# First block in four plain units, the second block's attention in the loop: a rewritten opening

## The chip, the cores and the metric

The kernel runs on one core of a Trainium2 chip. The metric is the device time of one execution in microseconds. Such a core has TensorE (PE, with weight loads listed apart as PEld), VectorE (DVE), ScalarE (ACT), GpSimd (POOL) and SyncE (SP), which here only issues the transfers of the DMA engines.

## What is computed

Attention over windows, and then two expert layers, all in float32. The core of the reference:

```python
for c in range(768 // 32):                       # windows of 32 queries, 16 left, 8 right
    k_full = concat([mem_k, k[:, :, l_start:r_end]])
    scores = scale * q_c @ k_full.T;  a = exp(scores - max);  a = a / (sum(a) + 1e-9)
    out[:, :, c_start:c_end] = a @ concat([mem_v, v_ctx])
x = out.reshape(3072, 512)                       # 4 batches x 768 tokens, 8 heads x 64
h = x @ w_in;  x = (h * sigmoid(1.702 * h)) @ w_out               # 512 -> 2048 -> 512
out = (silu(x @ w_gate) * (x @ w_val)) @ w_out2                   # 512 -> 1536 -> 512
```

The weights come as 64-bit floats and are turned into float32 on the chip.

## The kernel before

**Tiles.** The 3072 tokens are six blocks of 512, each of four groups of 128. Attention goes by group: queries (256 KB), keys and values with their windows laid out (512 KB each). The layers go by block and unit: a unit of the first layer is 256 columns of its hidden size (eight units), one of the second layer 128 (twelve). Every matrix product is made three times in float32r, with operands split into a high and a low half (high x high, high x low, low x high).

**A unit.** `unit` makes the two 128-column parts of a unit with seven products of 256 columns instead of eight (sums of weights `s12`, `s34` and of tokens stand in for the eighth). A plain unit (`plain_up`) makes them with two banks of twelve products of 512 columns and needs no token sums, but the untouched weights `a`, `a21`, `v`. After the gate, `down` adds the unit's part of the output in four steps `d`, six products of 512 columns each.

**Order of blocks.** `seq` gives each layer two passes over all blocks. In the first pass of the first layer block 0 takes two units (`PLAIN`) and each other block four; the second pass takes the rest. Units 0 to 3 stay in SBUF for the whole first pass. From `n = 2` on, the loop spreads the attention of the next block over the four units (`PLACES`); a unit's down steps run inside the next units (`chunk`).

**The opening.** Until the loop's first unit all engines and SP's queue follow a hand-written order, the string `OPENING`. A name is a step and a number: `ldq`, `ldk`, `ldv`, `ldw` load queries, keys, values and raw weight blocks; `sc`, `mx`, `ex`, `sm`, `ra`, `rc`, `wg`, `te`, `ec`, `pv`, `xf`, `st` are the attention of a group, scores to store; `hi` and `xl` split its result; `pr`, `cs`, `ct` turn a raw block into float32 (ScalarE, then two steps on VectorE); `wa`, `wb`, `wv`, `wo` cast high halves on ScalarE and the names with `l` behind them make low halves on GpSimd; `sumA`, `sumB`, `hiA`, `loA`, `hiB`, `loB` make the sums of weights and split them. `ua`, `ub` are the two half passes (six products of twelve) of a plain bank; `th`, `gt`, `gc`, `rs` are its gate; `dn`, `dm` the down steps of units 0 and 1. `tc`, `tl`, `ts` split and sum the tokens of block 1. The old opening also writes out units 0 to 2 of block 1 in seven products (`qa` to `qg` and the rest), and the attention of groups 0 to 11. Each engine runs its own names in that order; a DMA that waits for a buffer holds up all that is behind it on SP.

**Buffers.** Raw blocks (512 KB) 0 to 2 and from 7 on take any free one of three buffers (`RB`), blocks 3 to 6 lie in spare weight slots. Block 1, 3, 9 and 13 also hold the sums of their unit until these are split. A unit's blocks are {0, 1; 4, 5}, {2, 3; 6, 7}, {8, 9; 10, 11}, {12, 13; 14, 15}. Before, the keys of groups 0 to 7 have eight buffers of their own (`k_open`); later groups share `kbd`, so their load waits for the scores of the group ahead.

**Weights later.** New weights are made a step at a time between products; `pace` divides the steps left by the slots until a unit is due, and `give_w` frees slots after a unit's last use (`final`).

Of the kernel before, what the change touches and what calls it, by code (L numbers as in the profile page):

```python
# [19 lines left out]
P = 128  # L20
# [23 lines left out]
PLAIN = 2  # L44
# [13 lines left out]
def tile_attention_moe_moe(  # L58
# [198 lines left out]
    def split_lo(w, f, o=0, n=512):  # L257
        nc.gpsimd.tensor_sub(w[:, 1, o : o + n], f, w[:, 0, o : o + n].bitcast(F32))  # L258
# [24 lines left out]
    nraw, bits = [2 * len(AT)], {}  # L283
# [79 lines left out]

    ready = {(1, u) for u in range(2 * PLAIN)}

    def all_weights():
        for ph in (1, 2):
            for u in range(2 * PLAIN if ph == 1 else 0, UNITS[ph]):
                yield from weight_steps(ph, u)
        yield None  # L370

    weights = all_weights()
    need, made = [next(weights)], [40 * PLAIN]
# [16 lines left out]
    class Tokens:  # L390
# [10 lines left out]
        def sum(self, k):  # L401

            eng = self.engs[7 + k]
# [246 lines left out]
    SPARE = 14  # L650
# [6 lines left out]
    v_open = vm + [spare[12].bitcast(F32).rearrange("p (a c d) -> p a c d", a=HP, c=4)]  # L657
    ebd.append(spare[13].bitcast(F32).rearrange("p (a c e q) -> p a c e q", a=HP, c=4, e=2))
# [6 lines left out]
    def load_q(g):  # L665
        if g >= 2 * GRP or g % GRP < 2:
# [19 lines left out]
    def load_kv_first(n, g):  # L686
        if g >= 2 * GRP:
# [6 lines left out]
    def scores_first(g):  # L694
        if g >= 2 * GRP:
            at["k", g] = scores(g)
            return
# [10 lines left out]
    def exponents_first(g):  # L708
        if g >= 2 * GRP:
# [7 lines left out]
    def values_first(g):  # L717
        at["x", g] = values(g, bank("ps_v"), vm[g % 2] if g >= 2 * GRP else v_open[g % 3])
# [15 lines left out]
    def lo_x(g):  # L734
        eng, src = (V, at["x", g]) if g == GRP - 1 else (G, xq[g])
# [43 lines left out]
    def down_first(d):  # L779
        if "y" not in psum:  # L780
            s_ctx.close()
            psum["y"] = pool("ps_y", 1, PSUM)
        down(1, 0, 0, True, False, firsts[0], None, None, d, 0.5)

    def down_second(d):
        down(1, 0, 1, False, True, firsts[1], None, None, d, 0.5, held=full)

    full = {}

    def evict_first(d):  # L790
        full[d] = evict(full[d], None, d, 0.5)

    def store_first(d):
        nc.sync.dma_start(out=yp[0][:, d, :], in_=full.pop(d))

    seconds, un = [[] for _ in range(3)], [{} for _ in range(3)]
    QN = BLK // 2

    def quarter(bank_, part):
        return lambda u: un[u][bank_][:, part * QN : part * QN + QN]  # L800

    ca0, ca1, cb0, cb1 = quarter("a", 0), quarter("a", 1), quarter("b", 0), quarter("b", 1)

    def unit_product(new, out, w, o, k):
        def f(u):
            if new:
                un[u][new] = bank(f"ps_{new}")
            key, off = ((1, u, w), o) if w != "v" else ((1, u - u % 2, "v"), u % 2 * HALF)
            product(out(u), wt[key], off, tokens().ops[k], start=out is cb1 and k == 2 or new is not None)

        return f

    def unit_copy(name, src):
        def f(u):
            un[u][name] = cpool.tile([P, QN], F32, tag=name, name=name)
            nc.scalar.copy(un[u][name], src(u))

        return f

    def unit_add(out, name, src):  # L820
        return lambda u: V.tensor_add(out(u), un[u][name], src(u))  # L821

    def unit_curve(bank_):
        return lambda u: un[u].update({"t" + bank_: curve(un[u][bank_], 1)})

    def unit_gate(bank_):
        return lambda u: gate(un[u][bank_], un[u].pop("t" + bank_), un[u][bank_])

    def unit_cast(bank_):
        return lambda u: seconds[u].append(cast(un[u][bank_]))  # L830

    def unit_rest(bank_):
        return lambda u: rest(un[u][bank_], seconds[u]["ab".index(bank_) ^ 1])

    def unit_down(d):
        return lambda u: down(1, 1, u, u == 0, False, seconds[u], None, None, d, 0.5)

    def tokens():
# [29 lines left out]
        "wal": lambda u: split_lo(wt[1, u, "a"], bits[IN[u]]),  # L868
# [5 lines left out]
        "wbl": lambda u: split_lo(wt[1, u, "a21"], bits[IN[u] + 1][:, :HALF], 0, HALF),  # L874
# [233 lines left out]
```

## Time and profile before

| | |
|---|---|
| time, median of 3 runs | 1189.48 us (1189.32 to 1191.52) |
| the profiled execution's own time | 1190.33 us |
| its span, first to last instruction | 1188.6 us |
| TensorE busy | 1151.3 us (97%) |
| VectorE, ScalarE, GpSimd busy | 652.1, 568.1, 354.9 us |
| mean granted TensorE clock | 0.991 |

Times are from the span's start. A busy TensorE is not TensorE at its peak: products overlap, so the spacing of starts tells more than the mean duration. The clock is a share of full speed.

### The profile page before, as it was taken

How to read it: one execution, taken by the hardware profiler on the slowest of the kernel's cores; microseconds unless marked ns; L12 is line 12 of the kernel's file. 1: busy time of each engine (PE TensorE's matmuls, PEld its weight loads, DVE VectorE, ACT ScalarE, POOL GpSimd, SP SyncE). 2: the span in 40 equal slices, each digit the busy share in tenths (PEclk: the TensorE clock that was granted, in tenths of full speed). 3: DMA queues.
4: the chain of work that ended last, by engine and by line, in shares of the span. 5: the costliest groups of instructions: out<-in, count | busy, mean ns of one | idle time of the engine just before them, and what ended most of it. 6: DMA issues, size and time to landing. Idle time of an engine off the chain costs nothing.

```text
span 1188.6 us, 22301 instructions
## 1 busy us (share of the span) xinstructions
PE 1151.3 (97%) x8908; PEld 1039.6 (87%) x8908; DVE 652.1 (55%) x1117; ACT 568.1 (48%) x1185; POOL 354.9 (30%) x321
## 2 busy tenths in 40 slices
PE   4889999999999999999999999999999999999998
PEld 3778888888989999999988989999999999999997
DVE  5886756565765444443466564453556554453553
ACT  4866555455565454444455544343445544243342
POOL 4564221202454232321235433021345521021010
PEclk9889999999999999999999999999999999999999
DMA  9977354441454313322333321210225130320302
GB/s 304 296 253 231 110 157 120 130 140 63 137 166 118 106 66 114 131 74 62 106 116 107 106 99 36 72 71 1 89 89 178 36 103 5 107 92 15 107 25 83
DMA packets 62920, 131.47 MB, mean 111 GB/s; under 512 B 5728, under 2 KB 26208, under 8 KB 60512
## 3 DMA queue, kind: packets, MB, share of 16 engines
q1 hardware_dynamic: 62816, 130.05, 34.9%
q8 instruction: 70, 1.15, 0.4%
q14 instruction: 34, 0.28, 0.1%
HBM read 98.57 MB, written 31.46 MB: 109 GB/s over the span
## 4 chain that ended last, share of the span: by engine, by line
PE 86%; DMA 5%; DVE 3%; ACT 2%; issue 2%; POOL 1%; SPq 0%; DVEq 0%; ACTq 0%; POOLq 0%
PE y L585 35%; PE ps_a L450 27%; PE ps_c L450 12%; PE ps_b L450 9%; DMA raw<-in_wr 2%; PE ps_s L201 1%; PE ps_o L174 1%; DMA q<-in_qg 1%; DMA w<-in_kg 1%; DMA xd<-xf 1%; PE ps_t L158 1%; PE ps_v L174 1%; ACT ebd L167 0%; PE ps_u L546 0%; ACT g L551 0%
## 5 line engine op out<-in xcount | busy, mean ns | idle before, releaser
L450 PEld LDWEIGHTS ps_a<-b,w 128*128 128x128 f32 x2832 | 384.3, 189 | 39.6 <-DVE ps_a L502 4.2
L450 PE MATMUL ps_a<-b,w 128*128 128x256 f32 x2832 | 397.5, 283 | 5.7 <-DVE ps_a L502 2.1
L585 PE MATMUL y<-gs,w 128*128 128x512 f32 x1152 | 298.6, 395 | 0.6 <-DVE gs L565 0.5
L585 PE MATMUL y<-w,gs 128*128 128x512 f32 x864 | 247.7, 395 | 0.6 <-DVE gs L565 0.5
L585 PEld LDWEIGHTS y<-gs,w 128*128 128x128 f32 x1152 | 204.2, 189 | 36.2 <-DVE gs L565 1.4
L450 PE MATMUL ps_c<-b,w 128*128 128x256 f32 x1224 | 179.1, 282 | 0.0
L450 PEld LDWEIGHTS ps_c<-b,w 128*128 128x128 f32 x1224 | 167.1, 190 | 8.8
L585 PEld LDWEIGHTS y<-w,gs 128*128 128x128 f32 x864 | 144.2, 190 | 14.4 <-DVE gs L565 1.7
L258 POOL TENSOR_TENSOR w<-wf,w 128x512 fp32r<-128x512 f32 (+1 forms) x68 | 78.3, 1152 | 222.0 <-ACT w L255 221.9
L450 PE MATMUL ps_b<-b,w 128*128 128x256 f32 x900 | 135.5, 287 | 1.7 <-DVE ps_b L821 1.2
L450 PEld LDWEIGHTS ps_b<-b,w 128*128 128x128 f32 x900 | 120.4, 193 | 5.9 <-issue 1.7
L553 ACT ACTIVATE g<-ps_b 128x512 f32<-128x512 f32 x72 | 43.1, 598 | 166.1 <-DVE ps_b L508 166.1
L436 DVE TENSOR_TENSOR b<-xl,b 128x512 fp32r<-128x512 f32 x72 | 64.3, 893 | 80.4 <-ACT b L432 80.3
L502 DVE TENSOR_TENSOR ps_a<-m,ps_a 128x256 f32<-128x256 f32 x115 | 48.9, 426 | 104.0 <-PE ps_a L450 98.0
L492 ACT COPY u<-ps_a 128x256 f32<-128x256 f32 x115 | 43.0, 373 | 107.8 <-PE ps_a L450 107.6
L415 POOL TENSOR_TENSOR xl<-xl,t 128x512 f32<-128x512 f32 x18 | 23.3, 1296 | 231.3 <-DVE t L412 230.0
L565 DVE TENSOR_TENSOR gs<-ps_a,gs 128x512 fp32r<-128x512 f32 x118 | 80.8, 685 | 10.2 <-ACT gs L561 9.8
L487 DVE TENSOR_TENSOR ps_b<-p,ps_b 128x256 f32<-128x256 f32 x115 | 49.2, 427 | 61.3 <-PE ps_b L450 54.0
L561 ACT CAST gs<-ps_a 128x512 fp32r<-128x512 f32 x118 | 69.8, 592 | 22.5 <-DVE ps_a L531 15.6
L531 DVE TENSOR_TENSOR ps_a<-g,ps_a 128x512 f32<-128x512 f32 x72 | 50.0, 694 | 45.7 <-PE ps_a L450 45.2
L483 ACT COPY p<-ps_a 128x256 f32<-128x256 f32 x115 | 43.0, 374 | 60.3 <-PE ps_a L450 56.4
L508 DVE TENSOR_TENSOR ps_b<-u,ps_c 128x256 f32<-128x256 f32 x102 | 43.5, 426 | 50.1 <-PE ps_c L450 49.8
(123 smaller groups left out, 1190.6 us busy)
## 6 DMA issues: line engine op xcount, KB each, us to landing
raw<-in_wr SPq DMA_DIRECT2D x49, 512.0 KB, 3.4
xl<-yd SPq DMA_DIRECT2D x12, 1024.0 KB, 4.8
vm<-in_vg SPq DMA_DIRECT2D x22, 512.0 KB, 6.0
kbd<-in_kg SPq DMA_DIRECT2D x32, 256.0 KB, 4.2
raw<-in_wr SPq DMA_DIRECT2D x30, 256.0 KB, 5.3
yp<-o SPq DMA_DIRECT2D x24, 256.0 KB, 3.8
xl<-xd SPq DMA_DIRECT2D x6, 1024.0 KB, 4.8
base<-yp SPq DMA_DIRECT2D x24, 256.0 KB, 3.4
```

The costliest lines, as they stand in the source:

```text
L258: nc.gpsimd.tensor_sub(w[:, 1, o : o + n], f, w[:, 0, o : o + n].bitcast(F32))
L436: self.engs[k].tensor_sub(x[:, 1], self.source(k), x[:, 0].bitcast(F32))
L450: nc.tensor.matmul(ps, w[:, a, o + kc * P : o + kc * P + P], x[:, c, kc, :], start=(start and kc == 0 and (a, c) == PASSES[0]), stop=(kc = ...
L483: nc.scalar.copy(p1, ca[:, :n])
L487: add(cb[:, :n], p1, cb[:, :n])
L502: add(ca[:, n:], m, ca[:, :n])
L508: add(cb[:, n:], u2, cc)
L531: late[0] = [lambda: nc.vector.tensor_mul(ca, t, ca), lambda: gs.append(cast(ca))]
L553: nc.scalar.activation(t, c, AF.Silu)
L561: nc.scalar.copy(x[:, 0], g)
L565: nc.vector.tensor_sub(x[:, 1], g, x[:, 0].bitcast(F32))
L585: nc.tensor.matmul(y, lhs, rhs, start=(first and o == 0 and (a, c) == PASSES[0]), stop=(ends and o == len(gs) - 1 and (a, c) == passes[-1]),)
```

## The change

Block 0 takes four plain units in its first pass, all in the opening. Block 1's units all run in the loop, where `n = 1` now carries the attention of block 2 (groups 8 to 11). The opening keeps the attention of groups 0 to 7, all sixteen raw blocks and the weights of units 0 to 3, and ends where unit 0 of block 1 begins, with the token operands of block 1 split. Groups 4 to 7 take the later form of attention, with `kbd` and `vm` shared. Names can carry `/V` or `/G`: VectorE or GpSimd in place of the usual engine. The `a21` weights of two units share a tile, and the spare slots fall from 14 to 10.

```diff
-PLAIN = 2
+PLAIN = 4
...
-    spare_raw = [t.bitcast(I64) for t in spare[:4]]
+    spare_raw = [t.bitcast(I64) for t in spare[5:9]]
...
-    k_open += [spare[6 + i].bitcast(F32).rearrange("p (a c k) -> p a c k", a=HP, c=4) for i in range(6)]
+    k_open += [spare[i].bitcast(F32).rearrange("p (a c k) -> p a c k", a=HP, c=4) for i in range(2)]
...
     def load_kv_first(n, g):
-        if g >= 2 * GRP:
+        if g >= GRP:
...
     def scores_first(g):
-        if g >= 2 * GRP:
+        if g >= GRP:
...
-    def lo_x(g):
-        eng, src = (V, at["x", g]) if g == GRP - 1 else (G, xq[g])
+    def lo_x(g, eng=None):
+        src = at["x", g] if g == GRP - 1 else xq[g]
+        eng = eng or (V if g == GRP - 1 else G)
...
     def split_b(u):
-        wt[1, u, "a21"] = bpool.tile([P, 2, HALF], F32R, tag="b", name="a21")
-        split_hi(wt[1, u, "a21"], bits[IN[u] + 1][:, :HALF], 0, HALF)
+        if u % 2 == 0:
+            wt[1, u, "a21"] = wt[1, u + 1, "a21"] = bpool.tile([P, 2, BLK], F32R, tag="b", name="a21")
+        part_b(u, split_hi)
...
-    def down_second(d):
-        down(1, 0, 1, False, True, firsts[1], None, None, d, 0.5, held=full)
...
+            down(1, 0, u, u == 0, False, firsts[u], None, None, d, 0.5)
...
+        "dn": down_first(0),
+        "dm": down_first(1),
+        "do": down_first(2),
...
     OPENING = """
...
+        z0 tb0 z1 ldq0 ldk0 ldk1 ldq1 ldq2 ldv0 ldv1 ldk2 ldk3 sc0 ldq3 ldv2 mx0 sc1 ldq4 ex0 mx1 z2 ldw0 ldq5
+        sm0 ex1 sm1 ra0 sc2 rc0 ra1 wg0 ldw1 rc1 te0 wg1 mx2 te1 ec0 ldk4 sc3 ex2 ec1 sm2 pv0 mx3 ra2 pr0 ldw2
+        ex3 cs0 pv1 ldv3 ct0 xf0 hi0 st0 rc2 sm3 wg2/G wa0 ldw3 ra3 pr1 rc3 wg3 xl0 te2 xf1 cs1 hi1 st1 te3 ct1
+        ec2 ldw4 wal0 sc4 xl1/V wb0 pv2 ec3 sumA0 mx4 ldk5 pr2 wbl0 pv3 ldw5 hi2 sumB0 ldq6 xf2 hi3 xl2 cs2 hiB0
+        ua0 xl3 wv0 st2 pr3 ct2 ldv4 wvl0 xf3 ub0 ldv5 ex4 loB0 cs3 ldw6 wa1 ct3 ua1 th0 wal1/V sumA1 wv1 wb1
+        gt0 ua2 ldw7 pr4 st3 sm4 sumB1 gc0 ub1 ra4 rs0 pr5 ldw8 wbl1 cs4 hiA1 ub2 rc4 hiB1 wvl1 ct4 th1 loB1 cs5
+        ldw9 ua3 wo0 ct5 th2 wol0 gt1 wo1 sc5 gt2 gc1 wol1 ub3 pr6 ldk6 rs1 gc2 cs6 wg4/G ldq7 dn0 pr7 rs2 th3
+        ct6 te4 hiA0 cs7 dn1 wo2 loA0 mx5 ec4 wol2 dn2 ct7 pr8 gt3 wo3 ldw10 pv4 cs8 wol3 gc3 ct8 pr9 dn3 ldv6
+        rs3 wa2 ldw11 cs9 xf4 sc6 wal2 ct9 ex5 st4 dm1 ldq8 sm5 wv2 sumA2 ldk7 wb2 mx6 ra5 dm2 pr10 sumB2 hiA2
+        rc5 ua4 ex6 wg5 wbl2 hiB2 cs10 te5 pr11 wvl2 loB2/V ub4 loA2 ec5 cs11 ldw12 ct10 ua5 th4 ct11 ldw13 wo4
+        gt4 sc7 wo5 wol4 ldw14 sm6 gc4 ub5 ldk8 mx7 ra6 wol5 dm0 rc6 ex7 rs4 wg6/G th5 sm7 pv5 pr12 gt5 ra7 dm3
+        cs12 ldv7 gc5 rc7 xf5 rs5 wg7/G te6 pr13 st5 ct12 do1 ec6 cs13 ldw15 ct13 te7 pr14 do2 loA1/V wv3 sumA3
+        ec7 pv6 wvl3 wb3 pv7 tc0 wbl3 ldv8 xf6 tl0/V sumB3 ua7 xf7 ldv9 st6 tc1 ts0/G st7 do0 pr15 tl1/V wa3 ts1
+        ub7 wal3/V hiA3 hiB3 cs14 ua6 ts2/G ct14 th7 cs15 wo6 loB3 ct15 ub6 gt7 wo7 wol6 wol7/V tc3 th6 tl3/G
+        tc2 gt6 tl2/V gc6 loA3 gc7 rs6 ts3/G rs7 tc5 tl5 tc4 tl4/V tc6 tl6
     """
...
-    late[0] = [lambda: unit_rest("b")(2), lambda: unit_gate("a")(2)]
...
-        steps = attention(b + 1) if attends and n > 1 else []
+        steps = attention(b + 1) if attends and n else []
...
-            if n == 1 and u < 3:
-                gs = seconds[u]
-            elif n:
+            if n:
                 gs = unit(ph, u, ops, chunk, after, n < NBLK - 1, ph == 1 and ua > 0, nxt is None and last)
```

## Rows read from the trace of the kernel before

**Rows 1.** The page's first two parts: TensorE, its clock, the DMA engines.

```profile
PE 1151.3 (97%) x8908; PEld 1039.6 (87%) x8908; DVE 652.1 (55%) x1117; ACT 568.1 (48%) x1185; POOL 354.9 (30%) x321
...
PE   4889999999999999999999999999999999999998
...
PEclk9889999999999999999999999999999999999999
```

**Rows 2.** Windows: stretch, length, busy us of each engine, clock, DMA share, GB/s.

```profile
2.00:28.00 26.00, 10.49 (x369) 8.57 (x372) 14.23 (x27) 11.52 (x26) 9.32 (x11) 0.97 1.05 323
28.00:70.00 42.00, 36.37 (x622) 29.69 (x607) 36.21 (x58) 32.58 (x66) 25.94 (x26) 0.86 1.04 318
70.00:85.00 15.00, 12.07 (x95) 10.23 (x91) 11.10 (x15) 7.22 (x16) 11.12 (x9) 0.77 0.51 158
85.00:106.00 21.00, 21.00 (x225) 17.79 (x225) 13.98 (x25) 14.55 (x29) 8.94 (x10) 1.00 1.03 303
106.00:116.38 10.38, 9.16 (x58) 8.09 (x57) 7.85 (x14) 6.57 (x13) 4.52 (x4) 1.00 0.58 161
116.38:126.94 10.56, 10.56 (x68) 9.53 (x67) 6.64 (x10) 5.92 (x13) 6.82 (x5) 1.00 0.01 3
126.94:182.94 56.00, 54.76 (x539) 47.09 (x538) 34.82 (x61) 29.13 (x61) 13.31 (x13) 1.00 0.50 142
182.94:237.96 55.02, 54.51 (x539) 47.13 (x538) 33.51 (x58) 27.57 (x58) 7.28 (x6) 1.00 0.47 135
```

**Rows 3.** TensorE in order of time, opening: start, length, line, instruction, what it waited for.

```profile
27.50 1.18 PE L706 MATMUL ps_k<-w,q 64*32 64x64 f32 x64 [3.83 <-DMA w<-in_kg]
...
42.10 1.66 PE L546 MATMUL ps_u<-xh,w 128*128 128x512 f32 x6
...
47.68 0.60 PE L158 MATMUL ps_t<-ident,e 128*128 128x128 f32 x4
...
113.64 2.91 PE L585 MATMUL y<-gs,w 128*128 128x512 f32 x12
116.38 0.88 PE L450 MATMUL ps_a<-b,w 128*128 128x256 f32 x6
```

**Rows 4.** TensorE in order of time, attention inside the loop's units.

```profile
137.99 0.60 PE L158 MATMUL ps_t<-ident,e 128*128 128x128 f32 x4
138.52 1.08 PE L201 MATMUL ps_s<-kbd,q 128*32 128x128 f32 x32
139.53 1.69 PE L450 MATMUL ps_a<-b,w 128*128 128x256 f32 x12
...
144.73 1.15 PE L174 MATMUL ps_o<-ebd,vm 128*64 128x64 f32 x32
145.81 0.98 PE L450 MATMUL ps_b<-b,w 128*128 128x256 f32 x6
```

**Rows 5.** Windows of single microseconds in which the clock is at half.

```profile
27.00:28.00 1.00, 0.50 (x37) 0.51 (x40) 0.00 (x0) 0.07 (x1) 1.00 (x2) 0.50 1.08 301
38.00:39.00 1.00, 1.00 (x18) 0.88 (x16) 0.97 (x3) 0.27 (x2) 0.01 (x1) 0.50 1.07 374
78.00:79.00 1.00, 0.58 (x2) 0.58 (x3) 1.00 (x3) 0.00 (x0) 0.61 (x1) 0.50 0.01 2
83.00:84.00 1.00, 1.00 (x7) 1.00 (x7) 0.45 (x2) 0.00 (x0) 1.00 (x1) 0.50 0.70 213
```

**Rows 6.** VectorE and GpSimd in order of time: joins of words, one GpSimd subtraction.

```profile
31.90 0.68 DVE L301 SCALAR_TENSOR_TENSOR wf<-raw,wf 128x512 int32<-128x512 int32 x1
...
61.66 1.67 DVE L301 SCALAR_TENSOR_TENSOR wf<-raw,wf 128x512 int32<-128x512 int32 x1
...
61.44 1.34 POOL L258 TENSOR_TENSOR w<-wf,w 128x512 fp32r<-128x512 f32 x1 [0.69 <-ACT w L255]
```

**Rows 7.** GpSimd's late weight splits (units 4, 7), TensorE as unit 4 begins.

```profile
304.87 1.29 POOL L258 TENSOR_TENSOR w<-wf,w 128x512 fp32r<-128x512 f32 x1 [3.88 <-ACT w L255]
...
373.10 2.55 POOL L258 TENSOR_TENSOR w<-raw,w 128x512 fp32r<-128x512 f32 x2 [0.69 <-ACT w L255]
...
356.40 1.59 PE L450 MATMUL ps_a<-b,w 128*128 128x256 f32 x12
```

**Rows 8.** Waits of SP's queue in the opening: total us, times, longest.

```profile
SPq L119 <- PE ps_s L201: 10.2, 2, 7.2
```

More of the change, by code (lines that the diff above doesn't have):

```diff
@@ L281, in load_raw @@
                 nc.sync.dma_start(out=dst, in_=src[a])
[L283 removed]
+    nraw, bits = [4 * PLAIN], {}
     def take_words(i):
@@ L362, in weight_steps @@
         ready.add((ph, u))
-    ready = {(1, u) for u in range(2 * PLAIN)}
+    ready = {(1, u) for u in range(PLAIN)}
     def all_weights():
         for ph in (1, 2):
-            for u in range(2 * PLAIN if ph == 1 else 0, UNITS[ph]):
+            for u in range(PLAIN if ph == 1 else 0, UNITS[ph]):
                 yield from weight_steps(ph, u)
@@ L372, in tile_attention_moe_moe @@
     weights = all_weights()
-    need, made = [next(weights)], [40 * PLAIN]
+    need, made = [next(weights)], [20 * PLAIN]
     def prepare(n):
@@ L399, in __init__, with sum @@
             self.ops = [None] * 7
-        def sum(self, k):
-            eng = self.engs[7 + k]
+        def sum(self, k, eng=None):
+            eng = eng or self.engs[7 + k]
             if k == 0:
@@ L708, in exponents_first @@
     def exponents_first(g):
-        if g >= 2 * GRP:
+        if g >= GRP:
             exponents(g, at.pop(("k", g)))
@@ L717, in values_first @@
     def values_first(g):
-        at["x", g] = values(g, bank("ps_v"), vm[g % 2] if g >= 2 * GRP else v_open[g % 3])
+        at["x", g] = values(g, bank("ps_v"), vm[g % 2] if g >= GRP else v_open[g % 3])
     def group_cols(g):
@@ L777, in rest_first, with down_first, f @@
         rest(at.pop(("u", j)), firsts[j // 2][j % 2])
[L779 to L783, printed above, removed]
-    def down_second(d):
-        down(1, 0, 1, False, True, firsts[1], None, None, d, 0.5, held=full)
[L788 to L809, printed above, removed]
-        return f
[L813 to L836, printed above, removed]
+    def down_first(u):
+        def f(d):
+            if "y" not in psum:
+                s_ctx.close()
+                psum["y"] = pool("ps_y", 1, PSUM)
+            down(1, 0, u, u == 0, False, firsts[u], None, None, d, 0.5)
+        return f
     def tokens():
@@ L927, in tile_attention_moe_moe @@
-        pr5 st1 rc6 ex7 wg5 sumB1 ub0 hiA1 wg6 st2 xf3 loA1 ub1 cs4 hiB1 sm7 th0 ct4 wvl1 te5 st3 ra7 th1 ua2
-        loB1 ldw8 gt0 ec5 rc7 gt1 wbl1 ub2 gc0 wg7 pr6 rs0 ldw9 gc1 cs5 pv5 th2 rs1 pr7 gt2 sc8 wo0 ct5 gc2 wol0
-        pv4 ldk9 xf5 rs2 wo1 mx8 te7 ldv7 xf4 wol1 ldq10 te6 ec7 st4 cs6 ua3 st5 ct6 ex8 cs7 pr8 dn0 sm8 wo2 ct7
-        ra8 wol2 ub3 ec6 rc8 ldw10 wg8 wo3 pv6 cs8 th3 wol3 ct8 dn1 pr9 ldv8 gt3 ldw11 wa2 pv7 cs9 wal2 gc3 ct9
-        xf6 sc9 xf7 ldv9 rs3 sumA2 tc0 st7 ts0 te8 ldq11 tc1 dm1 ldk10 ts2 ts1 ec8 mx9 st6 dn2 tl0 tc3 ev1 pr10
@@ L1012, in tile_attention_moe_moe @@
                 tok = Tokens(xf.pop(nxt[1]), TE)
-            places = PLACES[u - ua] if n > 1 and attends else ()
+            places = PLACES[u - ua] if n and attends else ()
             def chunk(d):
```

89 lines of the change are left out of this document (24 added, 65 removed).

## The prediction

> **What bounds the kernel now.** I read the page's first two parts, then the windows of the opening and of the first blocks, then the instructions in order of time. The page has TensorE busy for 97% of the span, and its slices show the missing share in the first two or three only [rows 1]. The windows say the same with more precision: from 116.38 us on a plain unit of the first expert layer lasts 10.56 us with TensorE at 10.56 busy; before that point TensorE has gaps, the granted clock falls twice, and the DMA engines are full from 2 to 70 us and again from 85 to 106 us [rows 2]. So the kernel is a TensorE stream of fixed length behind an opening of 116.38 us, the start of the first unit that the main loop issues (block 1, unit 3) [rows 3]. The change rewrites the opening and moves work from it into the loop; the sum has to compare two lengths of opening against what the loop gains.
>
> **What the loop gains and loses.** After the change the opening ends where unit 0 of block 1 begins, with the same state of the pipeline (both times one of the four down steps of the last unit but one, and all four of the last, are still owed). The loop then runs four units of block 1 where it ran one, and these carry the attention of block 2. The first attending block of the loop, 126.94 to 182.94, took 56.00 us, the next 55.02 [rows 2]. I take 56.00, as it too follows the opening. It replaces one unit of 10.56: +45.44. Block 0's second pass loses two units of 10.56 each: -21.12. With T the end of the new opening,
> span = 1188.60 + (T - 116.38) + 45.44 - 21.12 = 1188.60 + (T - 92.06).
> The new opening must end by 92.06 us to pay. Nothing else in the first layer moves: of the remaining blocks each has the same units.
>
> **TensorE's work in the opening.** Twenty-four products of 512 columns, one plain unit, lasted from 42.10 to 47.68: 5.58 us. Twelve products of a down step lasted 113.64 to 116.38: 2.74, so a unit's 24 take 5.48, and the seven products of a unit in the loop take 10.56 - 5.48 = 5.08 [rows 2, 3]. (A plain unit is dearer by 0.5; two units turn plain, and this +1.0 is inside T below.) Of attention, a score takes 1.01, a transposition 0.53, a value product 1.08 [rows 4].
> Before, from the first plain product at 42.10 to 116.38, TensorE had 2 plain units (11.2), 3 in seven products (15.2), 3.75 downs (20.6), scores of groups 8 to 11 (4.0), 7 transpositions (3.7) and 8 value products (8.6): 63.3 us of work in 74.3. Stalls and the low clock of 77.7 to 84 us added 11.0, or 17%.
> After, behind the first plain product stand 4 plain units (22.3), 2.75 downs (15.1), three scores (3.0), four transpositions (2.1) and four value products (4.3): 46.8 us.
>
> **When the first plain product starts.** It needs group 3's values. Before, group 4's keys were the 18th transfer; with them 7.34 MB (ten transfers of 512 KB, eight of 256) had landed by 27.50 [rows 3]. After, group 3's values are at 7.86 MB, since weights stand behind them; at the 318 GB/s of the next 42 us [rows 2] that is 27.5 + 0.5/0.318 = 29.1 us. The value product (1.1) and two casts behind others on ScalarE bring about 33 us; 31.8 is the least, 36 if ScalarE's earlier waits for weight words add up. So 9 us of the old start are gained because the opening asks for attention first.
> From 33 us on, 46.8 x 1.17 = 54.8, so T = 87.8. The first passes also come into the stretch in which the clock was at half, 27 to 39 us [rows 5]; at half clock throughout, the two first half passes (2.8 us) would lose another 2.8; I take a quarter, 0.7, ends 0 and 2.8. T = 88.5. Without any stall it would be 31.8 + 46.8 = 78.6; from 36 us and with a quarter of stalls, 94.5.
>
> **The same from the transfers.** Group 7's keys are the last input that the opening's attention waits for. By then 17.83 MB are asked (27 transfers of 512 KB, 14 of 256): 27.5 + (17.83 - 7.34)/0.318 = 60.5 us if the queue never runs dry. It will once: raw block 9 needs one of three buffers, and these hold block 1 (until the low half of its first sums, `loA0`), block 7 (until `ct7`) and block 8. Both releases are written after `ub3`, which TensorE reaches at about 33 + 7 x 1.4 + 1.0 = 44 us unstalled and 46 with stalls; `th3`, `hiA0`, `loA0` or the DVE queue before `ct7` then bring 50 to 52 us. The transfers would have reached block 9 at 27.5 + (13.89 - 7.34)/0.318 = 48.1. Behind it on SP's queue stand the keys of groups 6 and 7, group 6's values and blocks 10 to 15; all of them come 3 to 4 us later, so group 7's keys land at 64 to 65. After these TensorE has one score (1.0) and 18.2 us more (five down steps, 6.9; three value products, 3.2; two transpositions, 1.1; five of the 16 half passes of plain units, 7.0): 64.5 + 1.0 + 18.2 x 1.17 = 86.8. The two routes agree within 2 us; I keep 88.5.
>
> **VectorE and GpSimd.** VectorE was busy 83.4 us before 116.38, GpSimd 59.8 [rows 2]. The opening sheds on VectorE four groups of attention (3.0 us each, 12), the additions and gates of the three units (6), evictions and token differences (4), four weighings that go to GpSimd (3), and takes five low halves (4.5): about 63 us, 76% of the time from 6 to 88.5 us, against 86% (36.2 of 42) from 28 to 70 before. GpSimd keeps about 58 us (weighings +5, low halves -6.5, two new ones +1.7, token work -2) and, since its first sums need the second weight block, does them from 22 us on: 87% of the time to 88.5, against 74% (11.1 of 15) in the fullest of the five stretches before. GpSimd is the engine that can spoil the sum, and ScalarE's in-order waits for words sit in the same chain.
> A join of words on VectorE took 0.68 us with GpSimd idle and 1.67 beside a GpSimd subtraction of 1.34 [rows 6]. The Trainium skill, SBUF — State Buffer, section "Who interferes with whom", says that a VectorE instruction with two SBUF inputs and a GpSimd instruction that reads SBUF share a port under a lock and that one of them blocks fully; the rows agree in size. It speaks against moving weighings to GpSimd while joins stay on VectorE. By the rows, 16 joins that each lose another 0.3 us cost 5 us of VectorE, not all on the path; that makes the second rival.
>
> **Smaller edits.** The tail of the opening splits all seven token operands; the third one needed (`tc3`, `tl3`) is written behind `ub6`. The first product of the unit needs only operand 0, written 20 names earlier; a loss there is part of the 17%. Scores of groups 4 to 7 take the 16-product form that groups 8 to 11 had: counted. Later, units 2 and 3 no longer stand between block 5's first pass and unit 4, so new weights are due 21.1 us sooner. Unit 4's last low half ended at 306.2, and unit 4 began at 356.4 + 0.7: hidden by 50 us, and by 29 after the change. The low halves of unit 7's two pairs of sums ended at 375.7 [rows 7]; unit 7 began 31.7 us after unit 4, at 388.8, and its first product with them comes 2.8 later, at 391.6. That is 16 us of cover; 21.1 sooner it lacks 5 to 6. But GpSimd works under half of that time, and the pacing divides the steps left by the slots to go, so it will make them sooner. I take 0.5, ends 0 and 6.
>
> **Sum.** 1188.6 + (88.5 - 92.06) + 0.5 = 1185.5, 3.1 less. The profiled execution's own time was 1190.33, 1.7 over its span and 0.85 over the median 1189.48. So 1189.48 - 3.1 = 1186.4 us. Within 0.2%, 2.4 us, is about what a measurement of this kernel cannot tell from no change.
>
> **Rivals.** (1) No change within 0.2%: GpSimd paces the opening. At 80%, halfway between what it did in its fullest stretch and what the forecast asks, 58 us of work take 72.5 from 22 us on; less its last two instructions (3 us), which are due after T, the opening ends at 91.5 and the time is 1189.4. For it: the 87% asked; against: its work is spread over the whole opening. (2) Slower: the keys of groups 4 to 7 now have one buffer, so each load waits for the scores before it, and SP's queue, with the weight blocks in it, stands still. Before, one such wait lasted 7.2 us [rows 8]; the DMA share was 0.51 from 70 to 85 us, and the clock fell in the same stretch [rows 2, 5]. Three loads of the new opening can meet it. One wait of that length on the path puts T at 88.5 + 7.2 = 95.7 and the time at 1193.6; it decides from T = 94.0, 5.5 us of standing queue. Against it: in my order the scores before each of these loads are done 8 us and more before the queue comes to the load. (3) Faster by 0.7%: the stalls shrink to 7%: T = 33 + 46.8 x 1.07 = 83.1, the time 1181. Against it: the two falls of the clock in the old opening.
>
> **Chances.** Forecast, with (3): faster by over 0.2%, T under 89.2: 0.51 (of it (3) 0.13). (1), T to 94.0: 0.28. (2): 0.21. The range takes T from 83.5 to 96.5: 1181.4 to 1194.4. The forecast's own range is 1183.5 to 1187.
>
> **What would show it.** Right: first plain product near 33 us, first unit of block 1 at 88.5, block 1's four units 56 us, block 0's second pass without two units, and a dip of DMA share near 50 us. Wrong: a unit of block 1 stretched by token operands, GpSimd full up to the last split, a clock at half for more than 6 us after 50, or a wait for weights at block 0's second pass.

## The result and the profile after

The changed kernel takes 1203.51 us (median of 4 runs, 1201.52 to 1204.60) where the kernel before takes 1189.86 (4 runs, 1189.32 to 1191.52): 1.011 times as long, 95% interval 1.0092 to 1.0129. The forecast was 1186.4 with a range to 1194.4. The change makes the kernel slower, by more than any of the cases that were priced.

The profiled execution took 1204.47 us with a span of 1202.7, 14.1 more than before. The first two parts of its page, in the lines that answer to [rows 1]:

```profile
PE 1156.0 (96%) x8744; PEld 1037.2 (86%) x8744; DVE 664.4 (55%) x1118; ACT 567.0 (47%) x1181; POOL 354.3 (29%) x320
...
PE   4897999999989999999999999999999999999998
...
PEclk9998999999999999999999999999999999999999
```

The totals show hardly a difference, and in the slices (30 us each) only the fourth has fallen, from 9 to 7; the third is fuller than before. Where the time went is seen in the stretches. TensorE in order of time (start, length, line, instruction, its idle time before) gives the ends that [rows 3] gave:

```profile
31.87 1.15 PE L174 MATMUL ps_v<-w,vm 128*64 128x64 f32 x32 [0.34 <-DMA vm<-in_vg]
33.48 1.88 PE L547 MATMUL ps_u<-xh,w 128*128 128x512 f32 x7 [0.46 <-ACT xh L726]
...
59.38 1.93 PE L201 MATMUL ps_s<-kbd,q 128*32 128x128 f32 x32 [3.17 <-DMA kbd<-in_kg]
...
89.93 0.88 PE L450 MATMUL ps_a<-b,w 128*128 128x256 f32 x6
90.64 0.88 PE L450 MATMUL ps_b<-b,w 128*128 128x256 f32 x6
91.36 1.55 PE L586 MATMUL y<-gs,w 128*128 128x512 f32 x6
99.29 1.65 PE L450 MATMUL ps_a<-b,w 128*128 128x256 f32 x6 [6.38 <-ACT p L483]
```

The first plain product stands at 33.48 (forecast: about 33), and the opening ends at 89.93 (forecast: 88.5; break-even: 92.06). So in this execution the opening itself pays 2.1 us, where 3.6 were planned. Nine microseconds later TensorE stands still for 6.38 us, inside the first unit that the loop issues. The windows of the same execution (length, busy us of the engines in the order PE, PEld, DVE, ACT, POOL, clock, DMA share, GB/s), beside [rows 2]:

```profile
45.00:50.00 5.00, 3.17 (x12) 1.74 (x10) 4.91 (x8) 3.13 (x6) 3.73 (x3) 1.00 0.39 103
50.00:55.00 5.00, 4.87 (x50) 3.98 (x51) 4.93 (x8) 4.03 (x8) 3.03 (x4) 1.00 0.24 66
...
89.93:111.47 21.54, 15.16 (x135) 12.66 (x134) 15.88 (x23) 10.37 (x21) 6.59 (x5) 0.84 0.51 144
111.47:153.20 41.73, 41.22 (x405) 35.44 (x404) 25.36 (x44) 22.25 (x46) 11.71 (x11) 1.00 0.53 154
153.20:210.50 57.30, 54.86 (x539) 47.11 (x538) 33.73 (x59) 27.93 (x58) 8.58 (x7) 1.00 0.46 129
210.50:266.50 56.00, 54.57 (x539) 47.19 (x538) 33.08 (x58) 27.59 (x58) 7.30 (x6) 1.00 0.46 133
266.50:321.17 54.67, 54.21 (x539) 47.21 (x538) 33.45 (x58) 28.11 (x59) 8.14 (x6) 1.00 0.34 98
321.17:413.48 92.31, 86.85 (x531) 75.79 (x530) 63.99 (x97) 55.53 (x113) 47.90 (x44) 1.00 0.49 148
```

From the starts of the units the 14.1 us add up. (A unit starts with the first of its products `ps_a`; two of these starts, 111.56 and 153.30, lie 0.1 us behind the cuts of the windows.)

| stretch | after | before, or forecast | difference |
|---|---|---|---|
| opening, to block 1's unit 0 | 89.93 | break-even 92.06 | -2.13 |
| block 1, four units (`n = 1`) | 63.37 | 56.00 | +7.37 |
| blocks 2 to 4 (`n = 2` to 4) | 167.86 | 165.71 | +2.15 |
| block 5's first pass, block 0's second pass | 92.31 for 8 units, 7.83 more than 8 x 10.56 | 106.7 for 10 units, 1.1 more | +6.73 |

Their sum is 14.12. What stands behind takes 789.2 us in both kernels. Block 1's units take 21.64, 15.02, 15.72 and 10.99. The first units of blocks 3 and 4 take 13.41, so block 1's first loses 8.2 us; the sum shows 7.4 for the block because the forecast's 56.00 already had losses of its own in it (units of 13.41, 15.53, 15.71 and 11.34).

**The first unit.** TensorE waits there for `p` (L483), ScalarE's first copy of the unit. ScalarE in order of time, around it:

```profile
89.78 0.62 ACT L255 CAST w<-wf 128x512 fp32r<-128x512 f32 x1 [1.77 <-DVE wf L301]
92.92 0.62 ACT L255 CAST w<-wf 128x512 fp32r<-128x512 f32 x1 [2.52 <-DVE wf L301]
93.44 0.61 ACT L432 CAST b<-t 128x512 fp32r<-128x512 f32 x1
...
96.79 0.63 ACT L432 CAST b<-xf 128x512 fp32r<-128x512 f32 x1
98.34 0.62 ACT L432 CAST b<-t 128x512 fp32r<-128x512 f32 x1 [0.92 <-POOL t L415]
98.87 0.36 ACT L483 COPY p<-ps_a 128x256 f32<-128x256 f32 x1
```

The products that `p` copies were done by 90.8. The copy, 8 us late, stands behind the written tail of the opening: casts `wo6` and `wo7`, which wait for VectorE's joins of blocks 14 and 15, the last plain unit's gates, and the casts of the last five of the seven token operands, the last of them behind GpSimd's sum `ts3`. VectorE and GpSimd in the same stretch (rows of both, each in its order):

```profile
86.54 1.51 DVE L296 TENSOR_SCALAR wf<-wh 128x512 int32<-128x512 int32 x1
88.09 1.66 DVE L301 SCALAR_TENSOR_TENSOR wf<-raw,wf 128x512 int32<-128x512 int32 x1
...
86.03 1.74 POOL L409 TENSOR_TENSOR t<-xf 128x512 f32<-128x512 f32 x1
...
95.37 1.72 POOL L258 TENSOR_TENSOR w<-raw,w 128x512 fp32r<-128x512 f32 x1
97.04 1.27 POOL L415 TENSOR_TENSOR t<-xf,t 128x512 f32<-128x512 f32 x1
```

So three queues close on one instruction. The granted clock is 0.51 from 98 to 103 us: it falls to half at 96.1, within the wait, and rises at 102.9, so that 3.6 us of products run at half. The wait of 6.4 and half of these 3.6 are the 8.2 us.

**Blocks 5 and 0.** TensorE never waits for a weight there. It waits for ScalarE's copy `p` (3.0 us), VectorE's additions into `ps_a` (1.7) and the operands of down steps (0.7), while VectorE's two steps of a weight block, shift (L296) and join (L301), have become longer. VectorE's groups by shape (busy us, mean ns) in that stretch, first after, then before:

```profile
L296 DVE TENSOR_SCALAR wf<-wh 128x512 int32<-128x512 int32 x15 | 15.2, 1015 | 8.6 <-ACT wh L288 4.7 <-POOL w L258 3.9
L301 DVE SCALAR_TENSOR_TENSOR wf<-raw,wf 128x512 int32<-128x512 int32 x15 | 12.5, 834 | 0.5
```

```profile
L301 DVE SCALAR_TENSOR_TENSOR wf<-raw,wf 128x512 int32<-128x512 int32 x15 | 11.0, 732 | 0.2
L296 DVE TENSOR_SCALAR wf<-wh 128x512 int32<-128x512 int32 x15 | 9.6, 640 | 6.4 <-ACT wh L288 5.2 <-POOL w L258 1.2
```

The same 30 instructions take 27.7 us where they took 20.6: 7.1 more, beside 6.7 lost. That the two are of one size shows no cause yet.

### The profile page after: what moved, and what is told of

It reads as the page before. It is cut to its first block, busy times and chain, and to the rows that moved or that the text cites. A ratio compares the mean times of both kernels' runs of the same rounds, so it can differ in the third digit from the quotient of the medians.

```text
span 1202.7 us, 21977 instructions
## 1 busy us (share of the span) xinstructions
PE 1156.0 (96%) x8744; PEld 1037.2 (86%) x8744; DVE 664.4 (55%) x1118; ACT 567.0 (47%) x1181; POOL 354.3 (29%) x320
## 4 chain that ended last, share of the span: by engine, by line
PE 78%; DVE 5%; ACT 4%; issue 2%; DMA 1%; POOL 1%; DVEq 0%; ACTq 0%; POOLq 0%; SPq 0%
PE y L586 31%; PE ps_a L450 25%; PE ps_c L450 11%; PE ps_b L450 8%; PE ps_o L174 1%; PE ps_s L201 1%; DMA xd<-xf 1%; DVE wf L296 1%; DVE wf L301 1%; DVE b L436 1%; ACT b L432 1%; ACT wh L288 1%; ACT w L255 1%; DVE t L412 1%; ACT gs L562 0%
## 5 line engine op out<-in xcount | busy, mean ns | idle before, releaser
L450 PEld LDWEIGHTS ps_a<-b,w 128*128 128x128 f32 x2784 | 377.5, 190 | 49.4 <-ACT p L483 12.7
L450 PE MATMUL ps_a<-b,w 128*128 128x256 f32 x2784 | 391.0, 283 | 13.9 <-ACT p L483 10.0
L586 PE MATMUL y<-gs,w 128*128 128x512 f32 x1152 | 302.6, 397 | 4.0 <-DVE gs L566 2.7
L450 PE MATMUL ps_c<-b,w 128*128 128x256 f32 x1200 | 175.7, 282 | 0.5 <-DVE gs L566 0.5
L450 PEld LDWEIGHTS ps_c<-b,w 128*128 128x128 f32 x1200 | 163.8, 190 | 9.5 <-DVE gs L566 0.9
L258 POOL TENSOR_TENSOR w<-wf,w 128x512 fp32r<-128x512 f32 (+1 forms) x65 | 75.8, 1167 | 199.0 <-ACT w L255 199.0
L450 PE MATMUL ps_b<-b,w 128*128 128x256 f32 x888 | 132.3, 285 | 0.0
L450 PEld LDWEIGHTS ps_b<-b,w 128*128 128x128 f32 x888 | 117.9, 191 | 4.5 <-issue 2.3
L554 ACT ACTIVATE g<-ps_b 128x512 f32<-128x512 f32 x72 | 43.1, 598 | 165.7 <-DVE ps_b L508 165.7
L566 DVE TENSOR_TENSOR gs<-ps_a,gs 128x512 fp32r<-128x512 f32 x116 | 79.5, 686 | 10.4 <-ACT gs L562 10.2
L483 ACT COPY p<-ps_a 128x256 f32<-128x256 f32 x116 | 43.4, 374 | 57.7 <-PE ps_a L450 54.0
```

Of the source, the lines that this page charges most:

```text
L258: eng.tensor_sub(w[:, 1, o : o + n], f, w[:, 0, o : o + n].bitcast(F32))
L450: nc.tensor.matmul(ps, w[:, a, o + kc * P : o + kc * P + P], x[:, c, kc, :], start=(start and kc == 0 and (a, c) == PASSES[0]), stop=(kc = ...
L483: nc.scalar.copy(p1, ca[:, :n])
L554: nc.scalar.activation(t, c, AF.Silu)
L566: nc.vector.tensor_sub(x[:, 1], g, x[:, 0].bitcast(F32))
L586: nc.tensor.matmul(y, lhs, rhs, start=(first and o == 0 and (a, c) == PASSES[0]), stop=(ends and o == len(gs) - 1 and (a, c) == passes[-1]),)
```

## Experiments

Each ratio is to the kernel before, timed on the same chip; T is the start of block 1's unit 0 in that run's profile, and "blocks 5 and 0" what their units lose over 10.56 us each (eight units, nine and ten with three and two plain ones). T is of one execution. In four profiles whose opening is the changed kernel's, untouched, it lies between 88.44 and 91.62, so differences of T under 3 us are not read.

**The copy first.** The tail's last names are issued inside the first unit, behind its first products (hook 0), its next ones (1) and later ones (3).

```diff
-        ... ct15 ub6 gt7 wo7 wol6 wol7/V tc3 th6 tl3/G
-        tc2 gt6 tl2/V gc6 loA3 gc7 rs6 ts3/G rs7 tc5 tl5 tc4 tl4/V tc6 tl6
+        ... ct15 ub6
...
+        0: "gt7 wo7 wol6 wol7/V tc3 tl3/G",
+        1: "th6 tc2 gt6 tl2/V gc6 loA3 gc7 rs6 ts3/G rs7",
+        3: "tc5 tl5 tc4 tl4/V tc6 tl6",
```

> Only the place of the opening's last 20 names changes: they are issued inside the first unit of block 1, behind its first copy (in three portions, after the first copy, after the first addition, after the second copy). Theory 'queue order': the first unit waited because its copy stood on ScalarE behind the token casts; the third product can then start when operand 3 is whole, about 95.5 us instead of 99.3, and the first unit lasts 16 to 18 us instead of 21.5: 1198 to 1200 us. Rival 'too much work': the tail is work of VectorE and GpSimd that must be done anyway, so the wait only moves to later products of the unit: 1202 to 1205 us, first unit 20 us or more.

1199.28 us, ratio 1.0079 (1.0059 to 1.0099). T is 88.35; the first unit takes 17.97 us instead of 21.64, block 1 59.56 instead of 63.37, and the wait for `p` is gone. TensorE in order of time, what is left:

```profile
89.78 1.55 PE L586 MATMUL y<-gs,w 128*128 128x512 f32 x6
92.53 0.39 PE L450 MATMUL ps_a<-b,w 128*128 128x256 f32 x1 [1.21 <-ACT b L432]
93.88 1.03 PE L450 MATMUL ps_a<-b,w 128*128 128x256 f32 x5 [0.96 <-POOL b L436]
```

So the queue's order was worth 3.8 us of the 7.4; now operand 3 itself is late, and the clock is at half from 94.4 to 97.8.

**The copy and operand 3 first.** Hook 0 then issues `tc3 tl3/G` ahead of `gt7 wo7 wol6 wol7/V`.

> As e1, and operand 3's cast and low half are issued ahead of the last output weight block. Queue order: both things that the third product waits for come by 93 us, so the wait of 6.4 us and the low clock behind it are gone: first unit 13.5 to 15.5 us, 1195 to 1197.5 us. Too much work: 1201 to 1204 us.

1199.49 us, 1.0084 (1.0068 to 1.0100), between the ranges of both theories: the first unit takes 17.51, the wait goes on to the operand of a down step, 1.98 us at 96.74.

**Words early.** The same, and `cs14 ct14` moved ahead of `tl0/V`, where VectorE had stood idle.

> As e2, and VectorE's shift and join of raw block 14 are issued ahead of the first token low half, where VectorE stood idle for 3.1 us. Queue order: up to 2 us less than e2, as that wait is already gone: 1194 to 1197 us. Too much work: idle time is filled, so 3 us less than e2: 1198 to 1201 us.

1205.08 us, 1.0122 (1.0103 to 1.0142): both theories missed. T is 94.14: the words now delay `wal3`, for which TensorE waits 2.69 us before 91.49. What was put into VectorE's idle place held up what came behind it.

**No words for 14 and 15.** The shift and join of the two last blocks are left out.

```diff
     def shift_words(i):
+        if i in (14, 15):
+            return
...
+        if i in (14, 15):
+            bits[i] = f.bitcast(F32)
+            return
```

> The changed kernel, with shift and join left out for raw blocks 14 and 15 alone (last output weights of the opening; the output is not the reference's). These four instructions took 6.4 us of VectorE just ahead of the tail's gates. If VectorE's queue sets when ScalarE's tail and the first copy come: the first unit loses 4 to 6 us of its wait and part of the low clock, 1196.5 to 1199.5 us. If GpSimd's token sums or the token casts set it: under 1.5 us, 1202 to 1204 us.

1202.21 us (1199.72 to 1204.43), 1.0106. TensorE still waits 4.63 us. ScalarE in order of time:

```profile
93.55 0.63 ACT L437 CAST b<-xf 128x512 fp32r<-128x512 f32 x1
97.18 0.62 ACT L437 CAST b<-t 128x512 fp32r<-128x512 f32 x1 [3.00 <-POOL t L420]
97.70 0.37 ACT L488 COPY p<-ps_a 128x256 f32<-128x256 f32 x1
```

Without VectorE's words ScalarE's queue stands 3.00 us for GpSimd's last token sum instead: two engines end at the same place, and to free one gives little (the time is not told apart from the changed kernel's).

**Weighings on VectorE.** `wg2`, `wg4`, `wg6` and `wg7` lose their `/G`.

> The changed kernel, with the four weighings that went to GpSimd back on VectorE. If GpSimd paced the opening, as the second rival of the prediction has it: its sums and splits come sooner, the opening ends 1 to 3 us earlier, 1200.5 to 1202.5 us. If VectorE's queue is the tighter one, as the tail suggests: 3 us more work there, the opening ends 1 to 3 us later, 1204.5 to 1206.5 us.

1204.09 us, 1.0121 (1.0106 to 1.0136). T 88.04, the first unit 21.59. No difference that these runs can tell: GpSimd's extra weighings, which stand in rival (1)'s sum, show no cost.

**Splits behind the tokens.** On top of the copy first, `tc3 tl3/G ts3/G` stand first in hook 0, and `hiA3 hiB3 loA3 loB3` go to a new hook 4.

> The first run's kernel; besides, GpSimd makes operand 3's low half and the last token sum right behind the other sums, and unit 3's splits of its two pairs of sums (due a block of work later) come behind these. If GpSimd's queue is what the tail's token operands wait for: the waits of 1.2 and 1.0 us of the third product go, the first unit lasts 14.5 to 16.5 us, 1196 to 1198 us. If VectorE's gates and rests of the last plain unit are as late: the wait moves to the down steps, 1198.5 to 1200.5 us.

1199.11 us, 1.0087 (1.0072 to 1.0102): as the copy first. The wait is at a down step again (1.97 us at 94.18).

**Three and two plain units.** On top of the copy first, `PLAIN` is 3 or 2, and the units left over run in block 0's second pass; the opening still makes the weights of all four.

```diff
-PLAIN = 4
+PLAIN = 3
...
-    nraw, bits = [4 * PLAIN], {}
+    nraw, bits = [16], {}
...
```

> The first run's kernel with three plain units in the opening; unit 3 is run in block 0's second pass (its weights are made in the opening as before). TensorE has 11.1 us less in the opening, the loop 10.6 us more, and the new weights get a unit of cover back (3 to 6 of the 7.8 us). If TensorE's own work paces the opening, as the prediction's sum has it: the opening ends 10 us sooner, 1193 to 1197 us. If transfers, VectorE and GpSimd pace it: it ends 0 to 4 us sooner, 1200 to 1206 us.

> As the run before with two plain units, as in the kernel before the change; units 2 and 3 are run in block 0's second pass and cover the new weights as they did. TensorE has 22.1 us less in the opening, the loop 21.1 us more. Paced by TensorE: 1190 to 1194 us. Paced by the others: the opening ends 2 to 8 us sooner, 1204 to 1212 us, and blocks 5 and 0 lose no more than before (1.1 us).

1201.73 (1.0108, 1.0093 to 1.0123) and 1211.91 us (1.0195, 1.0179 to 1.0210). T is 84.20 and 83.40: taking out two plain units, 22 us of TensorE's work, brings the end of the opening down by 5 only. With two, TensorE idles in it instead (3.33, 2.74 and 2.97 us are the longest waits between 60 and 69 us). With three, TensorE in order of time, in the first unit:

```profile
93.88 0.58 PE L450 MATMUL ps_a<-b,w 128*128 128x256 f32 x1 [4.76 <-ACT b L432]
95.50 1.43 PE L450 MATMUL ps_a<-b,w 128*128 128x256 f32 x5 [1.04 <-POOL b L436]
```

Operand 3 is whole at about 93.9 with four plain units in this order, 95.5 with three, and the first unit takes 23.68. With less work for TensorE it is the other engines, and when they have made the tokens, that decide. Blocks 5 and 0 lose 2.5 us with three and 1.1 with two, 7.83 with four: that loss depends on how many units are gone from their cover.

**No joins for units 4 to 7.** Their shift and join are left out.

```diff
-        shift_words(i)
-        yield 0
-        join_words(i)
+        if i < 2 * NF1:
+            bits[i] = bits[i][0].bitcast(F32)
+            yield 0
+        else:
+            ...
```

> The changed kernel, with the shift and the join on VectorE left out for the weights of units 4 to 7 of the first layer (their low bits are lost, so the output is not the reference's). Theory 'packed weight steps': blocks 5 and 0, in which these weights are now made within eight units instead of ten, lose their 7.8 us of stalls to VectorE's queue: 6 to 7 us less, 1196 to 1198 us. Rival: the stalls come from buffers or from GpSimd's splits, which stay: under 2 us less, 1201.5 to 1204 us.

1195.13 us, 1.0044 (1.0029 to 1.0059). All eight units take 10.56: the whole loss of that stretch hangs on these steps.

**Steps early in a unit.** `pace` issues steps only in the first half of a unit's slots, at a higher rate; and the same with the copy first.

```diff
-        credit[0] = min(credit[0] + want * (0.5 if turn else 11 / 9), 3.0)
+        credit[0] = min(credit[0] + want * (0.75 if turn else 11 / 6), 3.0)
...
-                if i > 1:
+                if 1 < i < 8:
```

> The changed kernel, with weight steps issued only in slots 2 to 7 of a unit, at a rate higher by 11/6 over 11/9, so that none stands between a unit's end and the next unit's first copy. If the 7.8 us of blocks 5 and 0 are lost because that copy queues behind weight steps (the waits named after the first copy are 1.95 and 1.08 us, the units around them lost 2.3 and 2.0): 4 to 6 us less, 1198 to 1200 us. If the sheer density of joins on VectorE is the cause, the waits move to the additions in mid unit: 1201.5 to 1205 us.

> The first run's order of the tail and the steps in slots 2 to 7 together. The two losses lie 200 us apart, so the gains add: 4.2 us from the tail and whatever the steps alone bring: 1194 to 1196 us if the copy's place is the cause, 1198 to 1200 us if it is density.

1213.15 (1.0202, 1.0181 to 1.0223) and 1208.47 us (1.0159, 1.0143 to 1.0175). Both are slower than either theory had it. Closer together the steps cost more: units up to 17.5 us, TensorE waiting 3.04 us at a time for `p`.

**Zeros for low halves.** GpSimd fills the low halves of units 4 to 7 with zeros instead of subtracting.

```diff
+        if low:
+            split_lo(w, f, o, n)
+        else:
+            nc.gpsimd.memset(w[:, 1, o : o + n].bitcast(F32), 0.0)
```

> The changed kernel, in which GpSimd does not compute the low halves of the weights of units 4 to 7 but fills them with zeros (so the products with these low halves are lost): GpSimd writes the same tiles at the same places of the order and reads nothing for them. VectorE keeps all shifts and joins. Port theory (the shifts of 1015 ns and joins of 834 ns on average in the blocks after 321 us are long because GpSimd's subtractions use SBUF beside them): the shifts come down to about 640 ns or less, the eight units of block 5's first pass and block 0's second pass lose 2.5 us or less where they lost 7.8, span 1197 to 1198, time about 1198.5. Queue theory (four steps for each raw block, packed into 21.1 us less, delay the gates on VectorE whatever GpSimd does): the durations may fall but the units still lose 6 us or more, span 1201 or more, time 1202 or more.

1196.24 us (1194.73 to 1200.27), 1.0046 (1.0029 to 1.0062). Blocks 5 and 0 lose 2.36 instead of 7.83; the profiled span, 1198.5, is of an execution whose opening ended at 91.62. VectorE's groups there:

```profile
L304 DVE SCALAR_TENSOR_TENSOR wf<-raw,wf 128x512 int32<-128x512 int32 x15 | 12.5, 835 | 0.5
L299 DVE TENSOR_SCALAR wf<-wh 128x512 int32<-128x512 int32 x15 | 8.0, 532 | 7.4 <-ACT wh L291 7.3
```

With every step of VectorE still in place, 5.5 of the 7.8 us go with GpSimd's subtractions, and the mean shift falls with them (1015 to 532 ns). Instruction by instruction: in the changed kernel eleven of the fifteen shifts ran beside such a subtraction and took 0.87 to 1.47 us; with the fills thirteen took 0.41 to 0.43. No join ran beside a subtraction of weights in either. Twelve took 0.69 in both, and three took 1.65, 1.66 and 0.89, in both, beside GpSimd's token instructions, which the fills left in place: so the joins keep their mean of 835. The port theory is borne out for the shifts; a fill is also shorter than a subtraction (0.49 against some 1.2 us), so that GpSimd reads and that it is busy longer aren't told apart.

**The copy first, without joins.** Both edits together.

> The first run's order of the tail, and no shift and join for the weights of units 4 to 7 (the output is not the reference's). The two losses are independent, so the gains of the two runs, 4.2 and 8.4 us, add: 1190 to 1192 us. If one hides part of the other: 1193 us or more.

1190.95 us (10 runs), 1.0012 (1.0002 to 1.0022). The two gains add (1190 to 1192 was expected), and with both the kernel stands near the kernel before, by the interval 0.02 to 0.22% slower.

**The store first.** On top of the copy first, the source stores a group's result ahead of the load of later values.

```diff
+        keep_x(g, ps)
+        store_x(g)
         if g + 2 < NG:
             load_kv("v", g + 2)
-        keep_x(g, ps)
-        store_x(g)
```

> The changed kernel with the opening's last names inside the first unit of block 1 (as in the run of the copy first), and in the loop each group's result is stored ahead of the load of the values two groups later, not behind it. Store theory (the last units of the third and fourth stretch of block passes wait 1.7 and 0.5 us for the down step's operand because VectorE's first token difference waits for the store, which lies behind a 512 KB load of values): the wait for the store at about 200 us falls from over 2 us to under 1, these stretches lose 1 to 2 us less, span 1195 to 1196. Rival (the store's own latency of 3.5 us sets it): span 1197 as in that run, the wait at about 200 us stays at 1.5 or more.

1199.94 us, 1.0079 (1.0064 to 1.0094). It tells nothing: the loads are still issued first (L115 at 191.96, the store L193 at 192.58), as the order of issue on SP isn't that of the source here. It stands as a repeat of the copy first, 0.7 us from it.

**The difference apart.** On top of the copy first, the loop's token results that overwrote the tokens get buffers of their own.

```diff
-                tok = Tokens(xf.pop(nxt[1]), TE)
+                tok = Tokens(xf.pop(nxt[1]), TE, True)
```

> The changed kernel with the opening's last names inside the first unit of block 1 (as in the run of the copy first), and with the loop's two token results that were written over the tokens themselves (the first difference on VectorE, which waits for the block's last store) in buffers of their own, so that nothing waits for the store. Store theory (that wait, 2.6 us at about 200 us, is what makes the last unit of the third stretch of block passes wait 1.7 us for its down step's operand): the wait for the store is gone, the units of blocks 2 to 4 lose 2 us less than in that run, span 1195 to 1195.5, time 1197 to 1198. Rival (ScalarE, whose casts of gates and tokens stand around the same place, or the four shared output buffers, set it as well): the units lose as much as in that run, span 1197 or more, time 1199 or more.

1196.08 us, 1.0050 (1.0035 to 1.0065). VectorE's first difference (L409) and TensorE behind it in the changed kernel, then VectorE in this one:

```profile
203.64 0.69 DVE L409 TENSOR_TENSOR xf<-xf 128x512 f32<-128x512 f32 x1 [2.46 <-DMA xd<-xf]
204.25 0.68 DVE L566 TENSOR_TENSOR gs<-ps_a,gs 128x512 fp32r<-128x512 f32 x1
...
204.99 0.73 PE L586 MATMUL y<-gs,w 128*128 128x512 f32 x2 [1.34 <-DVE gs L566]
```

```profile
196.61 0.69 DVE L409 TENSOR_TENSOR t<-xf 128x512 f32<-128x512 f32 x1
197.22 0.69 DVE L566 TENSOR_TENSOR gs<-ps_a,gs 128x512 fp32r<-128x512 f32 x1
```

The last units of blocks 1 to 4 take 10.56 us, and blocks 2 to 4 together 164.6 us instead of the copy-first run's 167.5. The in-place difference waited for the store of the tokens that it overwrites, and the operand of a down step stood behind it. It is the fastest version of the whole change, and still 0.5% slower than the kernel before.

What made that store late stands in the DMA view of its stretch: the changed kernel from 198.2 to 203.2 us, then the kernel before at the end of its block 3, 226.9 to 230.3.

```profile
q8 instruction: 1, 0.02, 1.2%
xd<-xf SPq DMA_DIRECT2D x1, 256.0 KB, 5.3
```

```profile
xd<-xf SPq DMA_DIRECT2D x1, 256.0 KB, 3.5
```

The queue `instruction` moved one packet of 16 KB, from 201.07 to 202.00. All but 33 of the store's packets were done by 201.5; these follow from 202.0 to 203.1. In fourteen profiles that overwrite in place such a packet starts among the store's, half a us or more before their end, at one block's end: the last unit then takes 11.9 to 12.5 us. Where none is within 1.5 us of the store the unit takes 10.9 to 11.0; one that ends in the first 0.8 us behind the store's issue goes with 10.9 to 11.9. With buffers of their own the units take 10.56 although such a packet is there (196.89 to 197.85).

**The same in the kernel before.**

> The kernel before, with the one edit that took the wait for the store away: the token results of the loop that were written over the tokens themselves go to buffers of their own. Store theory: the last units of the passes of blocks 1 to 3, which took 11.45, 10.98 and 10.67 us, all take 10.67, and some of the loss at their edges goes too: span 1187.2 to 1187.7, time 1188.5 to 1189.3, about 0.1% faster than the kernel before. Rival (there the store lands in time and other queues set the rest): span 1188.3 or more, no difference.

1189.32 us (11 runs) against 1189.54 (15 runs), 0.9993 (0.9984 to 1.0002). Its attending units take 164.6 us instead of 165.7, so the wait is gone there too; its profiled opening ended 1.7 later. The gain of about 1 us is not separated from no change.

## Why the prediction was wrong, point by point

**The opening.** "So T = 87.8" and "T = 88.5": 89.93 was measured, in the stated range of T (83.5 to 96.5) but above the 89.2 up to which the chances counted the forecast; the scatter of T (88.44 to 91.62) takes in that bound. The first plain product stands at 33.48, and the dip of the DMA share, 0.39 and 0.24 from 45 to 55 us, where the transfers' route put it. That route is what the trace shows: TensorE waits for group 6's keys until 59.38 and from there runs without a gap over 0.05 us to 89.93. Of the 9.7 us that stalls and clock add to 46.8 us of work (21%; forecast: 17% and 0.7 us), 5.2 are gaps, all before 59.4, and 3.4 are half of the 6.8 us, from 58.5 to 65.4, in which the clock was at half. The route that multiplies TensorE's work by 1.17 agreed by luck: with two plain units T is 83.40, 5 less than with four in the same order, where that route would take off 26 (two units of 5.58 + 5.48, times 1.17). VectorE's work was sized well, 63.0 us by the windows from 2 to 89.93 (forecast: about 63), GpSimd's too high, 51.8 (about 58). The opening's sixteen joins took 17.7 us, 2.9 more than before; the prediction priced 5 for them and announced a rival that it then did not list.

**Block 1: the first failed step.** "I take 56.00" and "The first product of the unit needs only operand 0 ...; a loss there is part of the 17%". 63.37 was measured. The prediction asked when an operand is needed, not what stands behind the tail: the unit's first instruction on ScalarE had its data at 90.8 and ran at 98.87, because it was issued behind the tail's casts. That is 3.8 us by the copy-first run. The other 3.6 are the late operand itself and the clock behind it; moving work within the tail (words early, splits behind the tokens, operand 3 first) only passed the wait on, and how to be rid of it stays open. Before, the same operands were made for a unit 0 at 70.2 us, inside the written order, and TensorE's waits beside them were 0.45, 1.00 and 1.17 us. The prediction, which asked for the cover of each edit, did not ask it of the hand-over from the opening to the loop.

**Later weights: the second.** "I take 0.5, ends 0 and 6": 6.73 was measured. The step reckoned with a wait of TensorE for weights, and none came. The pacing made them sooner, as the text said: the low halves of unit 7's sums ended at 393.5, 9.4 us ahead of the unit's start at 402.9 (before, by [rows 7], 13), and its last low half at 400.5 (before: 384.3, 4.5 ahead). But sooner means that the same 15 shifts and 15 joins share 8 units instead of 10, and that VectorE's steps meet GpSimd's subtractions more often: without the steps the loss is 0, without the subtractions 2.4. The bound of 6 was of the right size by another mechanism, and the value taken from it was wrong.

**"Nothing else in the first layer moves": the third.** Blocks 2 to 4 take 2.15 us more. Block 2's first unit loses 0.9, of which TensorE waits 0.65 for `p` (L483), ScalarE's copy again; the last units of blocks 2 and 3 take 12.21 and 11.81, before 11.34 and 10.88 (+1.8); block 2's second unit gives back 0.5. The last units rest on a store's landing, as the difference-apart run shows, and that landing on where a packet of the `instruction` queue falls: with three and two plain units, where none makes the stores of blocks 2 and 3 late, blocks 2 to 4 take 164.8 us with the in-place difference as it was. So this term is not set by the change alone.

**Rivals.** (1), GpSimd paces the opening: not so for its end, and the weighings show no cost, but its last token sum is one of the two queues behind the 6.38 us. (2), keys of groups 4 to 7: the wait for `kbd` lasted 1.5 us at most on SP, against 7.2 in [rows 8]; the longest wait there, 10.2, was for a raw block's buffer, released by a low half of GpSimd (L258), in kind as the forecast had it. (3), fewer stalls in the opening, did not come.

**Signs.** Of the signs of being wrong no wait for weights came, and GpSimd was busy for 41.3 of the 56.5 us behind the first plain product. Two were seen: a clock at half for more than 6 us after 50 (6.8 us from 58.5, and again from 96.1 to 102.9), and block 1's stretched unit. The second had no price and no chance of its own, and the packed weights were only the end, 6, of a small term.

**The sum.** The opening's gain against break-even is 2.1 us here, and 0.4 to 3.6 over the four profiles of it; it was bought with 16 (7.4, 6.7 and 2.2). With the copy first and the joins left out the profiled span is 1187.0, but that is the fastest of its ten executions, and their median is 0.1% over the kernel before.

## What to carry to other kernels

Where a written prologue hands over to a loop, price each engine's queue there and not only the data: here the loop's first copy had its data and waited 8 us for the last casts of the prologue on its own engine. When units are taken from a stretch, ask what was spread over them; a preparation that is still in time for its consumer may yet crowd the engines that feed the bound one. A tile that is overwritten in place waits for the store that reads it, and how late that lands can hang on what else the DMA engines carry.

## What was not expected of the hardware

A shift of VectorE (128x512, 4 bytes, one input) takes 0.42 us alone and 1.51 beside GpSimd's subtractions at 86.5 us; a join 0.69 and 1.66, much as in [rows 6]; GpSimd's own subtraction 1.27 and 1.74. The Trainium skill, SBUF — State Buffer, section "Who interferes with whom", says that a `tensor_scalar` in a two-port mode locks the pair of ports that GpSimd uses, and that two SBUF inputs contend with GpSimd's reads but not with its writes alone. Both fit what is measured here. The shifts fell to 0.41 to 0.43 us where GpSimd's subtractions became fills (in which mode they ran no run shows). The joins took 0.69 with no GpSimd instruction beside them and up to 1.66 beside those that read SBUF; a join beside a fill alone no run shows.

Behind a single 16 KB packet of the queue `instruction` the last 33 packets of a 256 KB store came 1.6 us after the others (203.1 against 201.5), and the unit that waited for the store took 12.21 us, where units with no such packet near took 10.9 to 11.0.
